# FNet and gated MLP on one core: the order of the last units of work, and when eight early chunks are split

## The chip, the cores and the metric

The kernel runs on one core of a Trainium2 chip. TensorE (PE) multiplies matrices, VectorE (DVE), ScalarE (ACT) and GpSimd (POOL) work on elements, and SyncE (SP) issues nearly all DMAs, in the order of its queue. PE writes into PSUM, which DVE and ACT read and GpSimd does not use here. The metric is device microseconds; the figure of merit is the median over several runs, here three for the kernel before.

## The reference, cut to what matters

```python
def _A_ref(x, dft_seq_re, dft_seq_im, dft_hid_re, dft_hid_im):
    a = jnp.einsum("bsd,ed->bse", x, dft_hid_re)
    b = jnp.einsum("bsd,ed->bse", x, dft_hid_im)
    return jnp.einsum("ts,bse->bte", dft_seq_re, a) - jnp.einsum("ts,bse->bte", dft_seq_im, b)

def _B_ref(x, w_gate, w_up, w_down):
    g = jnp.einsum("bsd,df->bsf", x, w_gate)
    u = jnp.einsum("bsd,df->bsf", x, w_up)
    h = _gelu(g) * u
    return jnp.einsum("bsf,fd->bsd", h, w_down)

h = x + _A_ref(_layernorm(x), ...)      # x is 1 x 2048 x 448, f32
h2 = h + _B_ref(_layernorm(h), ...)     # w_gate, w_up 448 x 1792, w_down 1792 x 448
```

Everything is f32 at the boundary. The change touches the second line alone, and in it the product of the gated hidden values with `w_down`, called "down" here.

## The kernel before, in words

Every f32 product is made from f16 halves: an operand is split into a high part (ACT rounds it to f16, `hi_part`, line 108) and a low part (DVE subtracts the high part from the value, `lo_part`, line 112), and PE runs three matmuls, high by high, high by low and low by high. On top of that the two products of the MLP use a seven-product scheme for 2 x 2 blocks, so that sums of blocks have to be formed before they are split.

The MLP runs in 42 **units** t = 0 to 41 of gate and up (`GateUp`), each for 128 of the 1792 hidden columns. Units 0 to 13 are for the first half of the rows, 14 to 27 for the third quarter and 28 to 41 for the last quarter. A unit accumulates in three PSUM banks, X, Y and Z, and its products are `x1`, `z1`, `y1`, `x2`, `z2`, `y2` and last `y3`, each 5 or 6 matmuls. `y3` is issued when the next unit has begun. Behind `z2`, `y2` and `y3` stands one DVE instruction each (lines 1076, 1084, 1089) that takes the sum out of its bank and so releases the bank. `c_last` is a Gelu on ACT and a product on GpSimd (line 1104). The hidden values of two neighbouring units lie in one SBUF tile `hs` of eight 128-column blocks, which `store` (line 1114) writes to DRAM after the odd unit, in the course of the next even one, or, for the last unit, after the loop.

Down runs in 56 **chunks** d = 7p + n. Group p = 0 to 7 stands for 256 rows of the output, and n = 0 to 6 for 256 hidden columns, those of the units 2n and 2n + 1 of a block. A chunk goes through: `hid_load` (SP reads it from DRAM into one of six tiles), `dn_sums` (three DVE instructions, lines 1174 to 1176), `dn_hi` (two on ACT), `dn_lo` (two on DVE), and `dn_mm` (21 matmuls, line 1212). The first of the two instructions of `dn_hi` and of `dn_lo` takes the chunk itself (128x256), the second its sums (128x640). Seven chunks accumulate in four PSUM banks. Then the group is **drained**: ACT copies two banks (`copy`, line 940), DVE adds four products from the others (`bank2`, `bank3`, line 944), GpSimd adds eight times from the copies (`sums`, line 972), and `dn_store` writes the 256 rows out (line 1230).

All of it is written out by hand, in one order per engine. The units 14 to 41 carry one or two chunks each (`steps`), so that in unit t the chunks of t are multiplied, those of t + 1 are split (`ahead`) and those of t + 2 are loaded and summed (`far`). The last two groups, p = 6 and 7, need hidden values of the units 28 to 41 themselves. Eight of their chunks are split during the units, into spare SBUF (`homes`): chunk `EARLY[t]` is loaded and summed in unit t - 1 and split in unit t + 1. The other six, 47, 48 and 52 to 55, are prepared just in time behind the loop, in the list `jit`, between the multiplications of the tail. Chunks 48 and 55 are made of the units 40 and 41. In the **tail**, PE multiplies chunks 42 to 52 one after the other, 11 times 21 matmuls, then products 0 to 6 of the chunks 53, 54 and 55, with DVE's last additions and the last stores between them.

What is scarce around the change: the accumulators of group 6 lie in the banks X, tr, Z and Y that the units leave, and the last three matmuls of a chunk go to Y (`dn_banks`, line 1195). Those of group 7 lie in the four banks of group 5. Chunks 47, 52 and 55 get one of three `dn_w` tiles, and 48, 53 and 54 one of two `raw` tiles, so that chunk 54 takes the place of chunk 48. A drain writes two tiles `v`, of which there is one set. At the end of unit 41 chunk 41 is multiplied, `y3` follows, and then the tail begins.

## Time and profile before

| | |
|---|---|
| median of three runs | 716.69 us (715.38 to 717.17) |
| time of the profiled execution | 715.99 us |
| span of the profiled execution | 714.2 us, 1.79 us less than its time |
| granted TensorE clock, mean | 0.997 |
| PE busy | 704.4 us, 99% of the span |
| DVE busy | 531.1 us, 74% |
| ACT, POOL busy | 353.0 us, 118.6 us |

The prediction quotes answers of the trace. A row of the timeline is start, duration, engine, line, operation, output<-input, shapes and count, and in square brackets the idle time of the engine before it with what ended it. PE rows of neighbouring matmuls of one kind are merged. A row of a table by window is the window, its length, the busy time and count for PE, PEld (weight load), DVE, ACT and POOL, then the granted clock, the busy share of the DMA engines and GB/s. A row of the waits is who waited for whom, the total, the number of times and the longest. A few matmul records are missing from the trace, so that counts can be short by some.

### The profile page before, as it was taken

The page shows a single profiled execution, that of the slowest core. Times are in us where ns is not written, and L with a number is a line of the kernel's source. Part 1 is how long each engine was busy: PE and PEld are TensorE (multiplying, and loading weights), DVE is VectorE, ACT ScalarE, POOL GpSimd, SP SyncE. Part 2 cuts the span into 40 slices and gives each one's busy share as a digit, 9 for nine tenths or more (in the row PEclk, how much of TensorE's full clock was granted, in tenths as well). Part 3 has the DMA queues.
Part 4 walks back from the last instruction along what each step waited for, and adds up shares of the span by engine and source line. Part 5 has one row for each costly group of instructions (what it writes and reads, how often), then busy time and mean ns, then how long its engine had stood idle before and what let it go on. Part 6 is the DMA issues. An engine that isn't in the chain of part 4 may idle for free.

```text
span 714.2 us, 13037 instructions
## 1 busy us (share of the span) xinstructions
PE 704.4 (99%) x4952; PEld 481.0 (67%) x4952; DVE 531.1 (74%) x1136; ACT 353.0 (49%) x656; POOL 118.6 (17%) x128
## 2 busy tenths in 40 slices
PE   9999999999999999999999999999999999999987
PEld 5555555555555555897644444479999999999877
DVE  7997648486858679998648787567688785989874
ACT  5776524163526354553527565554545544556421
POOL 0000000000000000000223333311231422334532
PEclk9999999999999999999999999999999999999999
DMA  7787538999988969552746858796898966878331
GB/s 271 250 248 264 113 135 240 235 311 247 235 299 248 243 214 266 216 137 86 191 159 225 289 193 193 198 339 229 226 310 244 278 243 231 314 266 312 121 116 52
DMA packets 116463, 160.47 MB, mean 225 GB/s; under 512 B 62000, under 2 KB 80560, under 8 KB 116400
## 3 DMA queue, kind: packets, MB, share of 16 engines
q1 hardware_dynamic: 116400, 159.64, 73.7%
q8 instruction: 38, 0.62, 0.4%
q14 instruction: 25, 0.20, 0.1%
HBM read 110.85 MB, written 34.87 MB: 204 GB/s over the span
## 4 chain that ended last, share of the span: by engine, by line
PE 97%; DVE 2%; DMA 1%; ACT 0%; issue 0%; SPq 0%; DVEq 0%
PE acc L648 33%; PE acc_d L1212 15%; PE pY L1010 14%; PE pZ L1010 9%; PE pX L1010 9%; PE y L714 9%; PE acc_f L520 7%; DMA wr<-in_w_seq_dram 1%; DVE dn_s L1175 0%; DVE dn_xs L112 0%; DVE hr L1476 0%; DVE hr L944 0%; DVE dn_s L1174 0%; DVE dn_s L1176 0%; DVE hs L1089 0%; ACT ws L108 0%
## 5 line engine op out<-in xcount | busy, mean ns | idle before, releaser
L648 PE MATMUL acc<-xs,ws 128*128 128x448 f16 x1248 | 237.9, 352 | 0.4 <-ACT ws L108 0.4
L648 PEld LDWEIGHTS <-ws 128*128 128x128 f16 x1248 | 122.0, 98 | 114.4 <-ACT ws L108 0.5
L1010 PEld LDWEIGHTS <-gw 128*128 128x128 f16 x1365 | 133.4, 98 | 42.9
L1212 PE MATMUL acc_d<-wd,dn_w 128*128 128x224 f16 x1008 | 111.0, 259 | 1.2 <-DVE dn_w L112 1.2
L1212 PEld LDWEIGHTS <-dn_w 128*128 128x128 f16 x1008 | 96.7, 98 | 3.7 <-DVE dn_w L112 1.7
L1104 POOL TENSOR_TENSOR hs<-hs,c 128x256 f32<-128x256 f32 (+1 forms) x42 | 53.6, 1277 | 226.7 <-ACT c L1102 159.1
L1010 PE MATMUL pY<-hops,gw 128*128 128x256 f16 (+1 forms) x595 | 89.9, 294 | 0.0
L114 DVE SCALAR_TENSOR_TENSOR ws<-wr,ws 128x1024 f16<-128x1024 f32 (+2 forms) x66 | 75.1, 1141 | 10.0 <-ACT ws L108 9.9
L108 ACT ACTIVATE ws<-wr 128x1024 f16<-128x1024 f32 (+2 forms) x66 | 63.8, 981 | 23.0 <-DMA wr<-in_w_seq_dram 21.9
L220 POOL TENSOR_TENSOR wd_s<-wd 128x448 f32<-128x448 f32 x7 | 9.4, 1349 | 343.3 <-DMA wd<-in_w_down_dram 342.5
L714 PE MATMUL y<-wh,z 128*128 128x448 f16 x336 | 66.2, 352 | 0.0
L1010 PE MATMUL pX<-hops,gw 128*128 128x256 f16 (+1 forms) x385 | 61.7, 294 | 0.0
L1010 PE MATMUL pZ<-hops,gw 128*128 128x256 f16 (+1 forms) x385 | 61.7, 294 | 0.0
L714 PEld LDWEIGHTS <-z 128*128 128x128 f16 x336 | 32.9, 98 | 30.1
L520 PEld LDWEIGHTS <-ws 128*128 128x128 f16 x504 | 48.3, 98 | 0.9
L1010 PEld LDWEIGHTS <-gu_w 128*128 128x128 f16 x273 | 26.6, 98 | 31.9 <-issue 0.3
L1055 ACT ACTIVATE pY<-pX 128x256 f32<-128x256 f32 (+1 forms) x42 | 18.4, 439 | 59.7 <-PE pX L1010 59.3
L1020 DVE SCALAR_TENSOR_TENSOR c<-pZ,u 128x256 f32<-128x256 f32 (+1 forms) x42 | 21.4, 510 | 34.6 <-PE pZ L1010 21.5
L1066 ACT ACTIVATE u<-pY 128x256 f32<-128x256 f32 (+1 forms) x42 | 19.1, 454 | 54.6 <-PE pY L1010 54.5
L972 POOL TENSOR_TENSOR hr<-hr,v 128x224 f32<-128x224 f32 x56 | 42.5, 785 | 16.7 <-ACT v L940 16.2
L112 DVE TENSOR_TENSOR dn_w<-dn_s,dn_w 128x640 f16<-128x640 f32 x48 | 43.1, 898 | 2.2 <-ACT dn_w L108 2.1
L108 ACT ACTIVATE dn_w<-dn_s 128x640 f16<-128x640 f32 x48 | 34.9, 728 | 18.9 <-DVE dn_s L1176 18.9
(133 smaller groups left out, 880.4 us busy)
## 6 DMA issues: line engine op xcount, KB each, us to landing
gw<-w_dram SPq DMA_DIRECT2D x35, 896.0 KB, 5.7
wr<-in_w_seq_dram SPq DMA_DIRECT2D x100, 256.0 KB, 4.5
hid_dram<-hs SPq DMA_DIRECT2D x28, 512.0 KB, 6.3
hid<-hid_dram SPq DMA_DIRECT2D x56, 256.0 KB, 5.7
w_dram<-gu_w SPq DMA_DIRECT2D x14, 896.0 KB, 5.7
gu_raw<-in_w_gu_dram SPq DMA_DIRECT2D x28, 384.0 KB, 5.8
wr<-in_w_seq_dram SPq DMA_DIRECT2D x14, 512.0 KB, 4.7
x<-in_x_dram SPq DMA_DIRECT2D x16, 224.0 KB, 2.7
```

The lines of the kernel that those rows point to most:

```text
L108: A.activation(dst, src, AF.Copy, scale=scale)
L112: V.tensor_sub(dst, src, hi)
L114: V.scalar_tensor_tensor(dst, src, scale, hi, op0=ALU.mult, op1=ALU.subtract)
L520: PE.matmul(fast_sum(n, k), fast_a(n, i, lw, a), fast_b(j, lx, b), start=j == 0 and m == 0 and k % 2 == 0, stop=j == NT // 2 - 1 and m == ...
L648: PE.matmul(acc[key][:, :D], w[:, lw, block * P : (block + 1) * P], xs[c][:, lx, :], start=c == 0 and m == 0, stop=c == NT - 1 and m == 2,)
L714: PE.matmul(y[:, :D], z[p][:, lz, k, g * P : (g + 1) * P], wh[:, lw, k, :], start=k == 0 and m == 0, stop=k == 6 and m == 2,)
L972: op(x, x, m)
L1010: PE.matmul(ps, w[:, wl, wa + ws, :], ops[:, m + ms, :], start=first and n == 0, stop=last and n == len(terms) - 1, skip_group_check=True,)
L1020: V.scalar_tensor_tensor(dst, ps, SC, other, op0=ALU.mult, op1=ALU.add)
L1066: A.activation(self.u2, self.Y, AF.Copy, scale=SC)
L1104: G.tensor_mul(c22, c22, self.cols(self.c12))
L1212: PE.matmul(ps, w[:, la, a, :], wd[n][:, lb, b, :], start=n == 0 and m == 0 and opens, stop=n == NC - 1 and m == 2, skip_group_check=True,)
```

## The change

It has four parts.

1. **The end of unit 41.** The drain of group 5 is not started in unit 41, and the splitting of chunk 46's low part, which stood ahead of `y3` on DVE, comes behind it. The sums of chunk 47 stay ahead of it.
2. **Chunks 48 and 55** are no longer stored and loaded back. `hid_in` of the two points into the `hs` tile of units 40 and 41. The last `store` and two `hid_load` are gone. `hid_load` of 53 and 54 moves from the tail into unit 41, behind that of 47 and 52. In `jit`, 48 now stands ahead of 52.
3. **The drain of group 5** (two copies on ACT, four additions on DVE) is issued behind the fourth chunk of the tail, and its eight GpSimd additions with the store behind the fifth. Before, the copies and additions of DVE stood in unit 41, and the GpSimd additions behind the first two chunks.
4. **EARLY.** Chunk 43 goes from 35 to 34, 50 from 36 to 35, 44 from 37 to 36, 51 from 39 to 37. Chunks 42, 49, 45 and 46 stay.

```diff
-    EARLY = {32: 42, 33: 49, 35: 43, 36: 50, 37: 44, 38: 45, 39: 51, 40: 46}
+    EARLY = {32: 42, 33: 49, 34: 43, 35: 50, 36: 44, 37: 51, 38: 45, 40: 46}
...
-        for d in far + ([52] if t + 1 == N_GU else []):
+        for d in far + ([52, 53, 54] if t + 1 == N_GU else []):
             hid_load(d)
...
         ends = now[-1] % NC == NC - 1
+        ends = ends and t + 1 < N_GU
         if ends:
...
-            if t + 1 < N_GU:
-                cur.z1()
+            cur.z1()
         prev.c_last()
         for d in ahead[1:]:
             dn_lo(d)
-        if split is not None:
+        if split is not None and t + 1 < N_GU:
             dn_lo(split)
...
     prev.y3()
-    prev.store()
-    hid_load(48)
-    jit = (47, 52, 48, 53, 54, 55, None)
+    hid_in[48], hid_in[55] = [hs[N_GU - 1][:, 4 * k : 4 * k + 4] for k in range(2)]
+    jit = (47, 48, 52, 53, 54, 55, None)
+    dn_lo(EARLY[N_GU - 2])
     for i, d in enumerate(range(6 * NC, 7 * NC + 4)):
         dn_mm(d)
-        if i == 0:
-            drains[5].sums(range(4))
         if i < 6:
             dn_hi(jit[i])
             dn_lo(jit[i])
             if jit[i + 1]:
                 dn_sums(jit[i + 1])
-        if i == 1:
-            drains[5].sums(range(4, 8))
-        if i < 3:
-            hid_load(53 + i)
-        if i == 2:
+        if i == 3:
+            drains[5] = dn_drain(5)
+            drains[5].copy()
+            drains[5].bank2()
+            drains[5].bank3()
+        if i == 4:
+            drains[5].sums(range(8))
             dn_store(5)
```

## Prediction, made before the changed kernel was built or run

> **What bounds the kernel now.** I read the page first, then the chain of waits of PE, then tables by window around each wait, and last the timeline of the engine that PE waited for.

> ```profile
> PE 704.4 (99%) x4952; PEld 481.0 (67%) x4952; DVE 531.1 (74%) x1136; ACT 353.0 (49%) x656; POOL 118.6 (17%) x128
> PE acc_d L1212 <- DVE hs L1089: 3.4, 1, 3.4
> PE acc_d L1212 <- DVE dn_w L112: 1.2, 1, 1.2
> ```

> PE is busy for 99% of the span, so an edit that leaves its matmuls alone can win only what PE waits, and these are the two waits in the part that the change touches. Around the longer one:

> ```profile
> 682.40:683.30 0.90, 0.90 (x10) 0.90 (x10) 0.90 (x2) 0.66 (x2) 0.90 (x3) 1.00 0.15 59
> 683.35:686.70 3.35, 3.35 (x21) 2.73 (x19) 2.88 (x6) 0.74 (x1) 1.15 (x1) 0.50 0.39 146
> ```

> After the wait the granted clock is 1.00 for 0.9 us, then 0.50 for 3.35 us. At half clock half of that is lost, 1.7 us. The wait therefore costs 3.36 + 1.7 = 5.06 us. The shorter one leaves the clock at 1.00:

> ```profile
> 667.00:670.00 3.00, 1.83 (x19) 1.46 (x17) 3.00 (x9) 2.23 (x6) 0.69 (x1) 1.00 0.36 141
> ```

> Why PE waited shows in the end of unit 41:

> ```profile
> 674.83 0.42 DVE L1020 SCALAR_TENSOR_TENSOR hs<-pY,m 128x256 f32<-128x256 f32 x1 [0.20 <-PE pY L1010]
> 676.48 1.61 DVE L944 SCALAR_TENSOR_TENSOR hr<-acc_d,hr 128x224 f32<-128x224 f32 x4 [1.23 <-PE acc_d L1212]
> 676.57 0.71 PE L1010 MATMUL pY<-hops,gw 128*128 128x256 f16 x5
> 677.12 1.89 PE L1212 MATMUL acc_d<-wd,hops 128*128 128x224 f16 x18
> 677.58 6.91 POOL L972 TENSOR_TENSOR hr<-hr,v 128x224 f32<-128x224 f32 x8
> 678.45 1.28 DVE L112 TENSOR_TENSOR dn_xs<-dn_s,dn_xs 128x640 f16<-128x640 f32 x1
> 679.65 0.88 DVE L1174 TENSOR_TENSOR dn_s<-hid 128x256 f32<-128x256 f32 x1
> 681.90 0.41 DVE L1089 SCALAR_TENSOR_TENSOR hs<-pY,g 128x256 f32<-128x256 f32 x1
> 682.37 3.76 PE L1212 MATMUL acc_d<-wd,hops 128*128 128x224 f16 x24 [3.36 <-DVE hs L1089]
> 683.90 0.87 DVE L1174 TENSOR_TENSOR dn_s<-hid 128x256 f32<-128x256 f32 x1
> ```

> `y3` ends at 677.3, but its DVE instruction, which releases bank Y, runs at 681.90. Ahead of it on DVE stand the drain of group 5, the low part of chunk 46 and the sums of chunk 47, these two slowed by the eight GpSimd additions (1.28 us for a form that takes 0.83 below). PE does 18 matmuls of chunk 42 and waits for Y until 682.37. The last row is for the pace under GpSimd work: a chunk takes 683.90 - 679.65 = 4.25 us on DVE.

> **The change, part by part.** *End of unit 41.* Ahead of `y3` on DVE only the sums of chunk 47 are left. Their price and the tail's pace come from a stretch in which GpSimd does nothing:

> ```profile
> 692.44 0.42 DVE L1174 TENSOR_TENSOR dn_s<-hid 128x256 f32<-128x256 f32 x1
> ...
> 693.31 0.42 DVE L112 TENSOR_TENSOR dn_w<-hid,dn_w 128x256 f16<-128x256 f32 x1
> 694.20 0.83 DVE L112 TENSOR_TENSOR dn_w<-dn_s,dn_w 128x640 f16<-128x640 f32 x1 [0.47 <-ACT dn_w L108]
> 694.94 0.42 DVE L1174 TENSOR_TENSOR dn_s<-hid 128x256 f32<-128x256 f32 x1
> ```

> Sums cost 0.87 us from start to start (692.44 to 693.31), a low part alone 0.42 + 0.83, at most 1.25 us, and a whole chunk just in time 2.50 us (692.44 to 694.94). The load of 47 must have landed, and it waits for the store of units 38 and 39:

> ```profile
> 668.14 0.32 SPq L1114 DMA_DIRECT2D hid_dram<-hs  x1
> 670.86 0.32 SPq L1127 DMA_DIRECT2D hid<-hid_dram  x1
> DMA to landing us min/median/max: 2.6/2.7/2.9
> ```

> It lands near 673.6 and does not delay them. So DVE takes sums 47 from 675.2 to 676.1 (677.0 if the GpSimd product of unit 41 doubles them), `y3` from 677.3 to 677.7, and Y is wanted at 677.12 + 1.89 = 679.0. The whole 5.06 us go; 1.3 us of DVE delay are in reserve.

> *Chunks 48 and 55 from SBUF, loads earlier.* A 512 KB store and two 256 KB loads go, 53 and 54 are issued on SP behind 52 with nothing queued behind them but the store of group 5. No wait of PE for these loads is in the chain of waits, so this gives nothing by itself. The sums of 48 now wait for `y3` and for GpSimd's product, both done by 678.

> *Tail.* Let PE start chunk 42 at 677.0 and do a chunk in 2.01 us:

> ```profile
> 696.64 0.42 ACT L108 ACTIVATE dn_w<-hid 128x256 f16<-128x256 f32 x1 [2.47 <-PE acc_d L1212]
> 698.40 2.17 PE L1212 MATMUL acc_d<-wd,dn_l 128*128 128x224 f16 x21
> 700.41 2.18 PE L1212 MATMUL acc_d<-wd,dn_xs 128*128 128x224 f16 x21
> ```

> DVE: low 46 to 678.9, low 47 to 680.1, then 2.50 us each for 48, 52 and 53 to 687.6, sums 54 to 688.5, the drain's 1.6 us (the L944 row) to 690.1. PE wants 47 at 687.0, 48 at 689.1, and group 5's banks for chunk 49 from 677.0 + 7 x 2.01 = 691.1 on, the fourth 18 matmuls (1.7 us) later. The moved drain is hidden with 1.0 us in hand. ACT then waits with `dn_hi(54)` until chunk 48 has freed its tile, as in the 696.64 row; behind it stand `dn_hi(55)` and the drain of group 6, in the old order too. From 691.1 two chunks take 5.0 us, or 8.5 at the pace under GpSimd work: chunk 55 is ready at 696.1 to 699.6 and wanted at 699.1 + 0.6. The eight GpSimd additions of group 5 (6.91 us before) run from 688 to at most 695, ahead of group 6's copies near 696, which need the same `v`. The tail costs nothing, and what follows PE's last matmul stays as it is.

> *EARLY.* Per unit, DVE gets the sums of 43 in unit 33 and its low part in unit 35; it loses sums in unit 38 and a low part in unit 40; the units between swap one chunk for another. DVE has no room early:

> ```profile
> 618.80:634.70 15.90, 15.88 (x155) 14.75 (x154) 15.90 (x33) 8.67 (x22) 7.84 (x11) 1.00 0.79 290
> 618.92 2.99 POOL L972 TENSOR_TENSOR hr<-hr,v 128x224 f32<-128x224 f32 x4
> 619.16 0.87 DVE L1175 TENSOR_TENSOR dn_s<-hid 128x256 f32<-128x256 f32 x1
> 620.62 0.41 DVE L1089 SCALAR_TENSOR_TENSOR hs<-pY,g 128x256 f32<-128x256 f32 x1
> 629.92 0.41 DVE L112 TENSOR_TENSOR dn_w<-hid,dn_w 128x256 f16<-128x256 f32 x1
> 630.39 0.31 PEld L1212 LDWEIGHTS <-dn_w 128*128 128x128 f16 x4 [0.27 <-DVE dn_w L112]
> 642.98 0.42 DVE L1020 SCALAR_TENSOR_TENSOR c<-pZ,u 128x256 f32<-128x256 f32 x1 [1.39 <-ACT dn_w L108]
> ```

> DVE is busy for all of 618.80 to 634.70, and chunk 32's low part (629.92) already holds PE's weight load at 630.39. The sums of 43 would stand at 620.62. They cost 0.87 us, or 1.9 if the GpSimd additions double them as they do at 619.16. One thing more can hold them: the load of 43 must wait for the store of units 30 and 31.

> ```profile
> 606.80 0.37 SPq L1114 DMA_DIRECT2D hid_dram<-hs  x1
> hid_dram<-hs SPq DMA_DIRECT2D x1, 512.0 KB, 7.7
> hid<-hid_dram SPq DMA_DIRECT2D x1, 256.0 KB, 7.1
> ```

> SP stands at that load until 614.5 (next in its queue is a load that issues at 616.78 anyhow), and the data lands 2.6 (the row above) to 7.1 us later, at 617.1 to 621.6: a wait of 0 to 1.0 us. All of it reaches chunk 32, since DVE has no gap on the way. PE loses 0.9 to 2.9 us near 630. I take 1.4, a half contended sum and no wait for the load. The low part of 43 in unit 35 (1.25 us) comes after chunk 32; the gap of 1.39 us at 642.98 takes it, and PE is itself later by then.

> Around the long wait the clock fell 0.9 us after PE had resumed (the 682.40 row), so a stretch in which PE still did something was idle enough. [...]

> *The wait at 668.* It is DVE's too:

> ```profile
> 654.01 3.37 POOL L1104 TENSOR_TENSOR hs<-hs,c 128x256 f32<-128x256 f32 x1 [6.48 <-ACT c L1102]
> 657.54 0.43 DVE L1020 SCALAR_TENSOR_TENSOR c<-pZ,u 128x256 f32<-128x256 f32 x1 [0.41 <-ACT dn_w L108]
> 658.20:670.80 12.60, 12.60 (x24) 1.00 0.47 161
> ```

> The sums dropped from unit 38 stood before 657.54, where DVE had caught up with PE, so they do not move what follows; from 658.20 DVE's work is the same. What they do is free GpSimd: its product took 3.37 us beside them, and the additions behind it, which slow DVE in unit 39, start earlier by a part of that. The wait of 1.17 us shrinks by 0 to 1.17; I take 0.7.

> **Sum**: 5.06 - 1.4 + 0.7 = 4.4 us less. Against the profiled execution's own time, 715.99 us, this is 711.6, against the median of three, 716.69, 712.3. I forecast 711.9, with 709.9 (5.06 - 0.9 + 1.17 off the profile, and the 0.7 us between profile and median once more) to 714.5 (5.06 - 2.9 off the median) as the likeliest case's own range.

> **Rivals.** *A, the new stall near 630 halves the clock.* A wait of 1.17 us did not; the one of 3.36 did, with at most 2.5 us of it in the 3.4 us before the fall. About 1.6 us lies between. Price 1.7 us: 713.6. *B, a new wait takes the old one's place: the drain of group 5 is late at chunk 49.* At 4.25 us a chunk, 48, 52 and 53 end at 692.9, the sums of 54 at 694.5 and the drain at 696.1. PE, which wants the fourth bank at 692.8, loses 3.3 us and 1.7 by the clock: 716.9. It decides once the drain ends after 692.8. For it speaks that the old tail did go at that pace; against it, that GpSimd's additions made it so, and they now come behind the drain. *C, slower, the change does not do what it says: the sums of 47 hold `y3`.* They stay ahead of it on DVE, and behind two transfers in a row. At the longest landings shown above the store of 668.14 lands 7.7 us and the load 7.1 us later, at 682.9, and Y is free after 0.87 + 0.41 us at 684.2. PE waits 5.2 us from 679.0, and 1.7 for the clock: 718.8. It decides once the load lands after 677.7. Against it: the store took 2.7 us there (668.14 to 670.86), the load as much, and the loads added stand behind it. *D, more gained*: DVE has more slack early than I see, and both short waits vanish: 5.06 + 1.17 + 0.27 off 716.3 (between the two bases) gives 709.8.

> **How the numbers follow.** The forecast has 0.69, A 0.10, B 0.07, C 0.06, D 0.08. About 0.3% (2.1 us) is what a measurement here tells from no change. Faster takes the forecast, D and half of A, 0.81; same the rest of A and most of B, 0.12; slower C and a little of B, 0.07. The range of 709.7 to 715.2 holds the forecast, A and most of D, and leaves out B and C.

> **What would show it.** PE's wait for line 1089 is gone and the clock stays 1.00 to the end; a PE wait for a low part of 1 to 2.5 us stands near 630; the wait near 668 is shorter than 1.17. The forecast is wrong if a wait of PE stands at chunk 42, 49 or 53 to 55, or if the clock falls before PE's last matmul.

## The result, and the profile after

| | before | after |
|---|---|---|
| median of five runs | 717.17 us (715.38 to 717.68) | 713.15 us (712.10 to 714.47) |
| profiled execution | 715.99 us | 712.20 us |
| its span | 714.2 us | 710.2 us |
| PE waits for line 1089 | 3.36 us, and 1.7 by the clock | none |
| PE waits near 630 and near 668 | 0.02 and 1.17 us | 1.67 and 0.69 us |

The ratio is 0.9947, with a 95% interval of 0.9928 to 0.9966: 2.4 to 5.2 us less, 4.0 by the spans. The forecast was 711.9 us, 4.4 us less than the profiled execution before.

The page of the changed kernel (busy time and share of each engine):

```profile
PE 703.0 (99%) x4952; PEld 480.1 (68%) x4952; DVE 531.8 (75%) x1136; ACT 353.2 (50%) x656; POOL 119.6 (17%) x128
```

And its waits (who waited for whom, in total, times, the longest); these two rows are all that PE has:

```profile
PE acc_d L1212 <- DVE dn_w L112: 2.4, 2, 1.7
PE pw L102 <- POOL sign_t L93: 1.4, 1, 1.4
```

PE's 4952 matmuls are the old ones, so what changed for PE are its waits and its clock. The 1.4 us lie at the start, in both kernels. What is left in the units are two waits for a low part, 1.67 and 0.69 us. The windows over the end of unit 41 and the tail, and over the wait near 630:

```profile
676.00:690.00 14.00, 14.00 (x148) 13.94 (x147) 11.68 (x26) 5.45 (x11) 2.31 (x3) 1.00 0.08 28
690.00:706.00 16.00, 16.00 (x170) 16.00 (x168) 10.56 (x26) 2.95 (x6) 9.48 (x15) 1.00 0.18 66
630.57:632.24 1.67, 0.00 (x1) 0.01 (x1) 1.67 (x7) 1.67 (x5) 0.00 (x0) 1.00 0.70 258
```

From 676 to 706, nearly to its last matmul, PE is busy without a gap at a clock of 1.00. Near 630 PE stands still for 1.67 us while DVE is busy throughout, and the clock stays. In the kernel before, the same place cost PE 0.02 us (0.92 busy of 0.94), for the weight load that it needs came just in time (630.39):

```profile
630.01:630.95 0.94, 0.92 (x10) 0.65 (x8) 0.94 (x2) 0.69 (x2) 0.00 (x0) 1.00 0.97 361
```

The timeline of the changed kernel shows why PE waits, first in the units:

```profile
619.12 3.44 POOL L972 TENSOR_TENSOR hr<-hr,v 128x224 f32<-128x224 f32 x4
620.83 0.41 DVE L1174 TENSOR_TENSOR dn_s<-hid 128x256 f32<-128x256 f32 x1
621.16 0.88 DVE L1175 TENSOR_TENSOR dn_s<-hid 128x256 f32<-128x256 f32 x1
622.63 0.41 DVE L1089 SCALAR_TENSOR_TENSOR hs<-pY,g 128x256 f32<-128x256 f32 x1
...
631.77 0.41 DVE L112 TENSOR_TENSOR dn_w<-hid,dn_w 128x256 f16<-128x256 f32 x1
632.24 0.56 PE L1212 MATMUL acc_d<-wd,dn_w 128*128 128x224 f16 x4 [1.67 <-DVE dn_w L112]
...
655.86 2.49 POOL L1104 TENSOR_TENSOR hs<-hs,c 128x256 f32<-128x256 f32 x1 [6.47 <-ACT c L1102]
658.32 2.63 POOL L972 TENSOR_TENSOR hr<-hr,v 128x224 f32<-128x224 f32 x4
670.49 0.56 PE L1212 MATMUL acc_d<-wd,dn_w 128*128 128x224 f16 x4 [0.69 <-DVE dn_w L112]
```

The sums of 43 take from 620.83 to 622.63, 1.80 us, doubled by the GpSimd additions of 619.12. Chunk 32's low part then stands at 631.77, 1.85 us later than before (629.92). PE's wait grows by 1.67 - 0.02 = 1.65 us; the other 0.20 us are a shift that PE has too, whose rows ahead of the wait are as much later (629.56 for 629.36). Near 655 the GpSimd product takes 2.49 us where it took 3.37, and the wait near 670 is 0.69. Then the tail:

```profile
676.53 0.42 DVE L1174 TENSOR_TENSOR dn_s<-hid 128x256 f32<-128x256 f32 x1
678.48 4.19 PE L1212 MATMUL acc_d<-wd,hops 128*128 128x224 f16 x42
678.75 0.42 DVE L1089 SCALAR_TENSOR_TENSOR hs<-pY,g 128x256 f32<-128x256 f32 x1 [0.73 <-PE pY L1010]
688.46 3.13 POOL L972 TENSOR_TENSOR hr<-hr,v 128x224 f32<-128x224 f32 x4 [10.93 <-ACT v L940]
688.73 0.88 DVE L1174 TENSOR_TENSOR dn_s<-hid 128x256 f32<-128x256 f32 x1
691.00 1.53 DVE L944 SCALAR_TENSOR_TENSOR hr<-acc_d,hr 128x224 f32<-128x224 f32 x4
692.57 2.18 PE L1212 MATMUL acc_d<-wd,hops 128*128 128x224 f16 x21
697.04 0.82 DVE L112 TENSOR_TENSOR dn_w<-dn_s,dn_w 128x640 f16<-128x640 f32 x1 [0.47 <-ACT dn_w L108]
```

The DVE instruction of `y3` (678.75) now waits for PE and no longer for other work on DVE. It releases Y at 679.2; PE wants it at 678.48 + 1.89 = 680.4. The moved drain runs at 691.00 to 692.53, just ahead of chunk 49 at 692.57. Chunk 55 is ready at 697.9.

By these rows the change is worth 5.06 - 1.65 + 0.48 = 3.9 us, and the spans say 4.0.

### The profile page after: what moved, and what is told of

Its sections match the earlier page's. It is cut to its first block, busy times and chain, and to the rows that moved or that the text cites. A ratio compares the mean times of both kernels' runs of the same rounds, so it can differ in the third digit from the quotient of the medians.

```text
span 710.2 us, 13038 instructions
## 1 busy us (share of the span) xinstructions
PE 703.0 (99%) x4952; PEld 480.1 (68%) x4952; DVE 531.8 (75%) x1136; ACT 353.2 (50%) x656; POOL 119.6 (17%) x128
## 4 chain that ended last, share of the span: by engine, by line
PE 95%; DVE 3%; DMA 1%; issue 0%; POOL 0%; SPq 0%; DVEq 0%; POOLq 0%
PE acc L648 33%; PE acc_d L1212 14%; PE pY L1010 14%; PE y L714 9%; PE pZ L1010 9%; PE pX L1010 9%; PE acc_f L520 7%; DMA hid<-hid_dram 1%; DVE dn_s L1175 1%; PE pw L102 1%; DVE dn_s L1174 0%; DVE dn_s L1176 0%; DVE dn_w L112 0%; DVE hops L112 0%; DVE hr L1476 0%
## 5 line engine op out<-in xcount | busy, mean ns | idle before, releaser
L1010 PEld LDWEIGHTS <-gw 128*128 128x128 f16 x1365 | 133.4, 98 | 42.9
L1212 PE MATMUL acc_d<-wd,dn_w 128*128 128x224 f16 x1008 | 111.2, 259 | 2.4 <-DVE dn_w L112 2.4
L1212 PEld LDWEIGHTS <-dn_w 128*128 128x128 f16 x1008 | 96.7, 98 | 5.2 <-DVE dn_w L112 3.2
L1104 POOL TENSOR_TENSOR hs<-hs,c 128x256 f32<-128x256 f32 (+1 forms) x42 | 55.3, 1316 | 225.1 <-ACT c L1102 150.3
L1010 PE MATMUL pY<-hops,gw 128*128 128x256 f16 (+1 forms) x595 | 89.9, 294 | 0.0
L108 ACT ACTIVATE ws<-wr 128x1024 f16<-128x1024 f32 (+2 forms) x66 | 63.8, 981 | 21.5 <-DMA wr<-in_w_seq_dram 20.8
L1010 PE MATMUL pX<-hops,gw 128*128 128x256 f16 (+1 forms) x385 | 61.7, 294 | 0.0
L1010 PE MATMUL pZ<-hops,gw 128*128 128x256 f16 (+1 forms) x385 | 61.7, 294 | 0.0
L1020 DVE SCALAR_TENSOR_TENSOR c<-pZ,u 128x256 f32<-128x256 f32 (+1 forms) x42 | 21.4, 510 | 37.8 <-PE pZ L1010 22.3
L1010 PEld LDWEIGHTS <-gu_w 128*128 128x128 f16 x273 | 26.6, 98 | 31.9 <-issue 0.2
L972 POOL TENSOR_TENSOR hr<-hr,v 128x224 f32<-128x224 f32 x56 | 41.8, 772 | 14.7 <-ACT v L940 13.8
L108 ACT ACTIVATE dn_w<-dn_s 128x640 f16<-128x640 f32 x48 | 35.0, 729 | 18.0 <-DVE dn_s L1176 18.0
L112 DVE TENSOR_TENSOR dn_w<-dn_s,dn_w 128x640 f16<-128x640 f32 x48 | 41.6, 867 | 2.0 <-ACT dn_w L108 1.9
## 6 DMA issues: line engine op xcount, KB each, us to landing
wr<-in_w_seq_dram SPq DMA_DIRECT2D x100, 256.0 KB, 4.5
hid_dram<-hs SPq DMA_DIRECT2D x27, 512.0 KB, 5.9
hid<-hid_dram SPq DMA_DIRECT2D x54, 256.0 KB, 5.6
wr<-in_w_seq_dram SPq DMA_DIRECT2D x14, 512.0 KB, 5.2
```

What stands on the lines that cost most here:

```text
L108: A.activation(dst, src, AF.Copy, scale=scale)
L112: V.tensor_sub(dst, src, hi)
L972: op(x, x, m)
L1010: PE.matmul(ps, w[:, wl, wa + ws, :], ops[:, m + ms, :], start=first and n == 0, stop=last and n == len(terms) - 1, skip_group_check=True,)
L1020: V.scalar_tensor_tensor(dst, ps, SC, other, op0=ALU.mult, op1=ALU.add)
L1104: G.tensor_mul(c22, c22, self.cols(self.c12))
```

## The experiments

Kernels of one group ran on one chip beside the same runs of the kernel before. "Changed" is the kernel of the result; each diff is against it unless another is named. All of them leave the computation as it is. The kernels with repeats do some sums several times over and write the same values.

### Is EARLY a loss by itself, and is the tail's gain whole without it?

The group's kernel before had a median of 716.63 us (714.75 to 719.50). The changed kernel once more, as the base:

> The changed kernel as it is, on the chip of the next three, so that they can be compared with it. Its trace had a span of 710.2 us with two waits of PE, 1.67 us near 632 and 0.69 us near 670. Both theories expect the same here: a span of 710 to 712 us, ratio to before 0.993 to 0.997, clock 1.00.

Measured: 713.53 us (712.78 to 713.88), ratio 0.995 (0.9937 to 0.9963), span 711.0, the waits 1.66 and 0.69 us.

The changed kernel with the old EARLY:

```diff
-    EARLY = {32: 42, 33: 49, 34: 43, 35: 50, 36: 44, 37: 51, 38: 45, 40: 46}
+    EARLY = {32: 42, 33: 49, 35: 43, 36: 50, 37: 44, 38: 45, 39: 51, 40: 46}
```

> The changed kernel with the old EARLY. Theory: the early units cost 1.67 - 0.21 = 1.46 us near 630 and give back 1.17 - 0.69 = 0.48 us near 670, and have no part in the tail. So the wait near 630 falls to about 0.2 us, the one near 668 is 1.2 us again, no wait stands in the tail, the clock stays 1.00, and the span is about 709.2 us, 1.0 less than with the new EARLY. Rival: the new EARLY takes work off VectorE in units 38 and 40 and thereby makes the room that the end of unit 41 needs; then a wait of 0.5 us or more stands at chunk 42, and the span is not below 710.2.

Measured: 711.45 us (711.08 to 712.33), ratio 0.9924 (0.9911 to 0.9937), span 709.8. The one wait for a low part that is left, in the timeline:

```profile
670.12 0.56 PE L1212 MATMUL acc_d<-wd,dn_w 128*128 128x224 f16 x4 [1.17 <-DVE dn_w L112]
```

The wait near 630 is gone and the one near 668 is back at its old 1.17 us. The other three parts alone gain 716.63 - 711.45 = 5.2 us (4.5 to 6.4 by the interval), and the first term of the sum was 5.06. EARLY gives back 2.1 us by the medians, 1.2 by the spans; the waits make 1.65 - 0.48 = 1.17 (the expectation took the old wait near 630 as 0.21 us; it is 0.02). The span with the old EARLY also holds a wait of 0.63 us for ACT near 349, in a part that EARLY does not touch and that half of the profiled executions here show. So some 0.7 to 0.9 us of what EARLY costs here are not explained by the two waits.

And the kernel before with the new EARLY alone:

> The kernel before with the new EARLY alone. Theory: span 714.2 + 1.46 - 0.48 = 715.2 us, about 1.0 us slower than before; the wait of 3.4 us for line 1089 and the half clock behind it stay. Rival: with less to do in units 38 and 40 VectorE reaches the last gated product earlier, the long wait shrinks by 1 us or more, and the span is 714 us or less.

Measured: 718.00 us (715.59 to 720.01, 12 runs), ratio 1.0021 (1.0007 to 1.0035): slower, by 0.5 to 2.5 us. Its profiled execution was the fastest of its twelve, and its trace holds something that no theory had. The wait for line 1089 is the old one:

```profile
616.57 4.27 POOL L1104 TENSOR_TENSOR hs<-hs,c 128x256 f32<-128x256 f32 x1 [4.83 <-ACT c L1102]
619.31 0.41 DVE L1174 TENSOR_TENSOR dn_s<-hid 128x256 f32<-128x256 f32 x1
631.50 0.56 PE L1212 MATMUL acc_d<-wd,dn_w 128*128 128x224 f16 x4 [0.99 <-DVE dn_w L112]
682.98 2.46 PE L1212 MATMUL acc_d<-wd,hops 128*128 128x224 f16 x24 [3.35 <-DVE hs L1089]
```

but the clock, by windows, stays at 1.00 behind it:

```profile
677.94:681.35 3.41, 1.69 (x18) 1.53 (x16) 3.31 (x6) 0.00 (x0) 3.33 (x5) 1.00 0.01 2
681.35:684.77 3.42, 1.79 (x19) 1.79 (x19) 3.42 (x6) 1.04 (x2) 3.42 (x5) 1.00 0.31 113
684.77:688.18 3.41, 3.41 (x38) 3.41 (x37) 2.32 (x5) 0.74 (x1) 0.34 (x1) 1.00 0.13 48
```

So the 1.7 us are not a fixed price of this wait. The section on the clock below goes on from here. In this trace the wait near 630 is 0.99 us and not 1.67: the sums of 43 ran undoubled, 619.31 to 620.18, while GpSimd's product took 4.27 us, where it took 2.52 in the trace of the changed kernel. The neighbour that yields was the other one this time.

### Which part of the tail removes the wait?

The group's kernel before: 717.22 us (714.68 to 719.51). First the drain of group 5 back in unit 41, its GpSimd additions behind the first two chunks:

```diff
-        ends = ends and t + 1 < N_GU
...
-            cur.z1()
+            if t + 1 < N_GU:
+                cur.z1()
...
-        if i == 3:
-            drains[5] = dn_drain(5)
-            drains[5].copy()
-            drains[5].bank2()
-            drains[5].bank3()
-        if i == 4:
-            drains[5].sums(range(8))
+        if i < 2:
+            drains[5].sums(range(4 * i, 4 * i + 4))
+        if i == 2:
```

> The changed kernel with the drain of group 5 back at the end of unit 41 (its GpSimd additions again behind the first two chunks of the tail); the low part of chunk 46 stays behind the last gated product, chunks 48 and 55 stay in SBUF. Theory: the drain's four additions hold VectorE until 679.4 (on the clock of the changed kernel's trace), the sums of 47 follow until 680.3, or 681.2 if GpSimd doubles them, and the last gated product's instruction ends at 680.7 to 681.6 where bank Y is wanted at 680.2: a wait of 0.5 to 1.4 us at chunk 42, no half clock, time 0.5 to 1.4 us above the changed kernel's. Rival: the low part of 46 was what held the product, so with it out of the way the drain may stay; no wait at chunk 42 and the same time.

Measured: 714.93 us (713.62 to 716.55), ratio 0.9965 (0.9945 to 0.9984). DVE's and PE's rows:

```profile
679.33 1.61 DVE L944 SCALAR_TENSOR_TENSOR hr<-acc_d,hr 128x224 f32<-128x224 f32 x4 [1.23 <-PE acc_d L1212]
680.86 0.51 DVE L1174 TENSOR_TENSOR dn_s<-hid 128x256 f32<-128x256 f32 x1
682.75 0.41 DVE L1089 SCALAR_TENSOR_TENSOR hs<-pY,g 128x256 f32<-128x256 f32 x1
683.22 2.46 PE L1212 MATMUL acc_d<-wd,hops 128*128 128x224 f16 x24 [1.36 <-DVE hs L1089]
```

The drain alone brings back 1.36 us of the wait, and the clock stays 1.00. A part of that is not the drain's own time: GpSimd's additions come back with it, at 680.43 in the same trace, and the sums of 47 beside them take 1.89 us (680.86 to 682.75) in place of 1.49. Second, the low part of 46 ahead of `y3` again:

```diff
-        if split is not None and t + 1 < N_GU:
+        if split is not None:
...
-    dn_lo(EARLY[N_GU - 2])
```

> The changed kernel with the low part of chunk 46 ahead of the last gated product again. Theory: VectorE is idle there for 0.81 us and the bank has 1.0 us more in hand, so 1.1 us of work (1.7 if GpSimd's product doubles it) fits: no wait at chunk 42, the same time within 0.3 us. Rival: each of the three pieces ahead of the product counts with its length, then a wait of 0.5 us or more appears at chunk 42.

Measured: 713.61 us (712.61 to 714.55), ratio 0.9947 (0.9927 to 0.9966), no wait at chunk 42. This edit alone is covered by the reserve: the low part fits by itself, and the drain does not. In the kernel before, both stand there, and the low part begins where the drain ends:

```profile
678.01 0.51 DVE L112 TENSOR_TENSOR dn_xs<-hid,dn_xs 128x256 f16<-128x256 f32 x1
```

It lasts to 679.65, 1.64 us, and the sums of 47 to 681.90, 2.25 us in place of 1.89. So 1.36 + 1.64 + 0.36 = 3.36 us: behind the drain nothing is left in reserve, and all that follows it counts in full.

Third, the store and the loads of 48 and 55, with the old order of the list:

```diff
-    hid_in[48], hid_in[55] = [hs[N_GU - 1][:, 4 * k : 4 * k + 4] for k in range(2)]
-    jit = (47, 48, 52, 53, 54, 55, None)
+    prev.store()
+    hid_load(48)
+    hid_load(55)
+    jit = (47, 52, 48, 53, 54, 55, None)
```

> The changed kernel with the hidden values of units 40 and 41 stored and chunks 48 and 55 loaded back from DRAM behind the last gated product, in the old order 47, 52, 48, 53, 54, 55; all else as changed. Theory: the store issues at 679.2, lands 2.7 to 4.8 us later and the load 2.7 to 3.8 us after that, at 684.6 to 687.8. VectorE, done with 52 at 684, waits with the sums of 48 for 1 to 4 us, and as the drain of group 5 stands two chunks behind them it ends at about 692 to 695 where chunk 49 wants the fourth bank at 694.3: a wait of PE of 0 to 1 us at chunk 49, time 0 to 1 us above the changed kernel's. Rival, as the prediction had it: the loads are hidden and give nothing by themselves; no wait at all and the same time.

Measured: 713.13 us (712.57 to 713.41), ratio 0.9942 (0.9927 to 0.9956), no wait of PE in the tail. The transfers do delay DVE and ACT, but ahead of work that has time:

```profile
685.57 0.42 DVE L1174 TENSOR_TENSOR dn_s<-hid 128x256 f32<-128x256 f32 x1 [1.35 <-DMA hid<-hid_dram]
```

The theory that they cost up to 1 us ends at zero within the noise; that these transfers are hidden, as the prediction had it, holds. The earlier loads of 53 and 54 were not taken back by themselves.

### Two waits that were left, and a faster version

The wait near 668 is DVE at the pace that GpSimd's additions leave it: with the old EARLY a low part of 128x640 takes 1.28 us beside them (663.91) and 0.81 behind them (669.99). The old EARLY, with group 4's eight additions moved to unit 40, where DVE has time (it idles for 3.37 us ahead of 673.28 in the trace of this kernel):

```diff
-    EARLY = {32: 42, 33: 49, 34: 43, 35: 50, 36: 44, 37: 51, 38: 45, 40: 46}
+    EARLY = {32: 42, 33: 49, 35: 43, 36: 50, 37: 44, 38: 45, 39: 51, 40: 46}
...
-            if p < 5 and t - t0 in (1, 2):
+            if p < 4 and t - t0 in (1, 2):
...
-            if p < 5 and t - t0 == 3:
+            if p == 4 and t - t0 == 3:
+                drains[p].sums(range(8))
+            if p < 5 and t - t0 == 3 + p // 4:
```

> As the run with the old EARLY, and the eight GpSimd additions of group 4 are moved from units 38 and 39 into unit 40, their store one unit later. Theory: the wait near 668 comes from these additions, which double VectorE's work in unit 39 (split and sums, some 3 us more), so it goes and the span is 709.2 - 1.2 = 708.0 us. Rival: VectorE has too much in unit 39 even without them, the wait stays at 0.5 us or more, or the additions now slow the sums of chunk 47 so that a wait of up to 1 us stands at chunk 42; span 709 us or more.

Measured beside the first group: 710.13 us (709.62 to 711.50), ratio 0.9906 (0.9892 to 0.9921), span 707.9. It is 1.3 us faster than the old EARLY alone, for a wait of 1.17. Behind the start PE has no wait at all any more in this trace. GpSimd's additions in their new place, in the timeline:

```profile
670.12 5.28 POOL L972 TENSOR_TENSOR hr<-hr,v 128x224 f32<-128x224 f32 x8
```

Once more, in the third group (kernel before 717.22, 714.15 to 719.84):

> The kernel with the old EARLY and the additions of group 4 moved to unit 40, again, beside the run above on the same chip. Both theories: no PE wait behind the start, 709.6 to 711.5 us.

Measured: 711.18 us (710.24 to 712.41), ratio 0.9926 (0.9901 to 0.9951). Its profiled execution has two waits of PE far from the change, 0.67 us near 350 and 0.16 near 480. This version beats both kernels. Then the same idea for the new EARLY, with group 3's additions in unit 36 and group 4's in unit 40:

```diff
-            if p < 5 and t - t0 in (1, 2):
+            if p < 3 and t - t0 in (1, 2):
...
-            if p < 5 and t - t0 == 3:
+            if (p, t - t0) in ((3, 4), (4, 3)):
+                drains[p].sums(range(8))
+            if p < 5 and t - t0 == (3, 3, 3, 5, 4)[p]:
```

> The changed kernel, new EARLY and all, with GpSimd's eight additions of group 3 moved from units 33 and 34 to unit 36 and those of group 4 from units 38 and 39 to unit 40, each store one or two units later. Theory: the new EARLY costs PE time only because GpSimd doubles VectorE's work in units 33, 34 and 39. Without that VectorE is some 4 us earlier at the low part of chunk 32 and 3 us earlier at that of chunk 40, so both waits near 632 and 670 are gone, no PE wait is left behind the start, and the time is that of the kernel with the old EARLY and the moved additions, 710 us. Rival: VectorE has too much to do in units 33 to 35 with the sums and the low part of 43 even alone; then a wait of 0.8 us or more stays near 632.

Measured: 712.42 us (711.85 to 713.73), ratio 0.9942 (0.9922 to 0.9961): the mechanism came out and the time did not. The sums of 43 are undoubled (621.04 to 621.91, 0.87 us) and both waits for a low part, near 630 and near 670, are gone. A new wait takes their place:

```profile
642.97 5.86 POOL L972 TENSOR_TENSOR hr<-hr,v 128x224 f32<-128x224 f32 x8
647.62 0.54 ACT L940 ACTIVATE v<-acc_d 128x448 f32<-128x448 f32 x1 [1.63 <-POOL hr L972]
648.22 0.73 PE L1212 MATMUL acc_d<-wd,dn_w 128*128 128x224 f16 x6 [1.49 <-ACT v L940]
```

There is one set of tiles `v`. The late additions of group 3 hold it, ACT's copies of group 4 wait, and PE waits for the bank that they read. The expectation had overlooked that.

### What does a wait cost by the clock?

To set the length of the wait, the sums of chunk 47 are done n more times ahead of `y3`, n = 4, 5 and 8:

```diff
+        if t + 1 == N_GU:
+            for _ in range(n):
+                h, s = dn_hid(47), dn_s[47]
+                V.tensor_add(s[:, 0:2], h[:, 0:2], h[:, 2:4])
+                V.tensor_sub(s[:, 2:4], h[:, 1:4:2], h[:, 0:4:2])
+                V.tensor_add(s[:, 4], h[:, 0], h[:, 3])
```

> The changed kernel with the three instructions of the sums of 47 issued four times more, with the same result, ahead of the last gated product: 4 x 0.87 = 3.5 us more work on VectorE at that place. Theory: 1.84 us of it fit (0.81 idle, 1.03 before the bank is wanted), so PE waits about 1.6 us at chunk 42, in one stretch; the clock stays at 1.00 since a stretch of 1.7 us left it there elsewhere; time 1.6 us above the changed kernel's. Rival: what decides the clock is the length of a wait alone with a limit somewhere between 1.2 and 1.6 us here, so the clock halves in this place and the time is 3.3 us above.

Measured: 714.44 us (713.92 to 714.80), ratio 0.996 (0.9948 to 0.9973), in the second group.

> The changed kernel with five repeats of the sums of 47 ahead of the last gated product (four gave a wait of 1.52 us and no fall of the clock). Wait 1.52 + 0.87 = 2.4 us. Theory: the clock falls when more than some share of one 3.41 us stretch of a fixed grid is idle, and that share lies between 1.73 us (no fall) and 2.45 us (fall). So a wait of 2.4 us halves the clock in a part of the executions at most, where nearly all of it lies in one stretch: times 715.9, or 717.6 with the fall. Rival: the length of the wait decides, with a limit between 1.67 and 3.35 us; then all executions are alike.

Measured: 716.73 us (715.45 to 717.79, 12 runs), ratio 1.000 (0.9986 to 1.0015), in the third group.

> The same with eight repeats: a wait of 1.52 + 4 x 0.87 = 5.0 us, of which at least 2.5 us lie in one stretch of 3.41 us whatever its phase. Theory: the clock falls in every execution and costs 1.7 us (3.4 where two stretches are idle enough): 713.5 + 5.0 + 1.7 = 720.2 us or more, with a spread no wider than that of a kernel without waits unless two stretches count. Rival, a stretch must be idle from end to end: with 5.0 us this holds in about half of the executions (1.6 of 3.4 us of phase), so the times fall into two groups, 718.5 and 720.2.

Measured: 720.16 us (719.76 to 722.91), ratio 1.006 (1.0038 to 1.0082), in the third group. PE's wait in the timeline, and then the windows from the start of the stretch that holds it, for four repeats:

```profile
682.38 1.79 PE L1212 MATMUL acc_d<-wd,hops 128*128 128x224 f16 x17 [1.52 <-DVE hs L1089]
```

```profile
679.89:683.30 3.41, 1.89 (x21) 1.72 (x19) 3.41 (x11) 1.04 (x2) 0.00 (x0) 1.00 0.00 0
683.30:686.71 3.41, 3.41 (x39) 3.41 (x37) 2.94 (x8) 1.04 (x2) 0.00 (x0) 1.00 0.03 7
```

The same two views for five:

```profile
683.82 4.12 PE L1212 MATMUL acc_d<-wd,hops 128*128 128x224 f16 x24 [2.40 <-DVE hs L1089]
```

```profile
680.73:684.14 3.41, 1.01 (x12) 0.85 (x10) 3.41 (x13) 0.68 (x2) 0.00 (x0) 1.00 0.01 2
684.14:687.55 3.41, 3.41 (x21) 2.77 (x19) 2.97 (x7) 1.11 (x4) 0.00 (x0) 0.50 0.02 5
```

And for eight:

```profile
685.41 4.64 PE L1212 MATMUL acc_d<-wd,hops 128*128 128x224 f16 x24 [5.02 <-DVE hs L1089]
```

```profile
680.62:684.03 3.41, 0.00 (x0) 0.00 (x0) 3.41 (x13) 0.00 (x0) 0.00 (x0) 1.00 0.00 0
684.03:687.45 3.42, 2.04 (x12) 1.66 (x12) 3.42 (x10) 1.04 (x2) 0.00 (x0) 0.50 0.02 5
687.45:690.86 3.41, 3.41 (x20) 2.79 (x19) 2.94 (x10) 1.04 (x2) 0.00 (x0) 0.50 0.00 0
```

The windows of the kernel before, cut in the same way:

```profile
679.92:683.33 3.41, 0.96 (x11) 0.96 (x11) 3.41 (x6) 1.04 (x2) 3.41 (x6) 1.00 0.04 17
683.33:686.74 3.41, 3.41 (x21) 2.79 (x19) 2.94 (x6) 0.74 (x1) 1.17 (x1) 0.50 0.39 144
```

In the three of these with a fall the clock changes at the ends of stretches of 3.41 us, which lie elsewhere in each execution (first change at 683.33, 684.14 and 684.03). It is halved for the next stretch where PE was idle for 2.40 us of a stretch (five repeats), 2.45 (before) or all of it (eight). It is not where PE was idle for 1.52 us (four repeats) or for 1.72 and then 1.63 (new EARLY alone, whose wait of 3.35 us was cut in two by a boundary). No change of the clock marks the stretches of the last two near the wait: their boundaries are an estimate, counted in the steps of 3.41 us of the other traces. So the bound, if the idle time of a stretch decides, lies between 1.72 and 2.40 us, an estimate from these five traces. With eight repeats the second stretch, idle for 1.38 us, was followed by half clock too: 2.04 us of work in it at half clock did not bring the clock back.

So four and five repeats, 0.88 us apart in PE's wait, are 2.3 us apart by the medians, though not on the same chip.

How often the clock falls can be read without a trace, because every execution of the experiments has its mean granted clock on record. One stretch at half clock takes 1.7 us of some 714, or 0.0024, off the mean. The traces give the scale: the mean is 0.999 or 1.000 where the clock did not fall, 0.997 with one such stretch (before, five repeats) and 0.995 with two (eight repeats). Executions by falls, each with its median time (0.998 counts as one):

| | none | one | two |
|---|---|---|---|
| kernel before, 50 | 18, 715.5 us | 26, 717.3 us | 6, 718.6 us |
| new EARLY alone, 12 | 2, 716.1 us | 10, 718.4 us | none |
| five repeats, 12 | 3, 715.8 us | 9, 717.2 us | none |
| eight repeats, 7 | none | none | 7, 720.2 us |

All other kernels here have 0.999 or 1.000 in every execution. So the fall does come in only a part of the executions with five repeats, as the theory had it, and the rival, by which all are alike, is out. It also bears on the new EARLY alone: with one fall each, it is 718.4 against 717.1 us for the nine such executions of the kernel before beside it, 1.3 us slower. Why the kernel before has two falls in 6 executions no trace shows.

## Why the prediction was right, and where it was off

- **The long wait, 5.06 us.** Right in its mechanism. The wait for line 1089 and the half clock are gone, and without EARLY the gain is 5.2 us. The price of the clock in it was right for the profiled execution, and the prediction took it as the wait's own. New EARLY alone shows an execution with the same wait and no fall, and of 50 executions of the kernel before 18 have none. That the profiled one has one is luck for the sum: without it the term would have been 3.36 us.
- **The reserve at `y3`, 1.3 us.** Measured 680.4 - 679.2 = 1.2. The sums of 47 take 1.5 us from start to end and are early enough; rival C, the late load, did not come.
- **EARLY, a new wait of 1.4 us.** Measured 1.67 - 0.02 = 1.65. The mechanism was right to the chunk, and nearly all of the delay reached PE, as the step had it. The size is low because the sums were doubled in full, 1.80 us, where the step took a half contended sum; the load did not hold them. New EARLY alone shows that this could have gone the other way (0.87 us).
- **The wait near 668, 0.7 us less.** This term is mis-sized too: 1.17 - 0.69 = 0.48. The product near 655 became 0.88 us shorter, as the step had it (3.37 to 2.49), and about half of that reached PE.
- **The tail costs nothing.** Right by its result, with a step that failed. The prediction had GpSimd's additions behind the drain in rival B and from 688 on in its own step, and it priced DVE's sums of 54 beside them as if GpSimd did nothing. They follow ACT's copies and began at 688.46, ahead of these sums and of the drain. The sums took 2.27 us (688.73 to 691.00) in place of 0.87. Carried to the later start of chunk 42, 678.48 in place of 677.0, the drain was to end at 691.6; it ended at 692.53, with 0.04 us in hand ahead of chunk 49 and not 1.0. PE wants the last bank 1.7 us later still, so it did not wait, and rival B stayed away by less than it seemed.
- **Chunks 48 and 55, nothing.** Right: with their transfers back the time is 713.13 us.
- **Rival A.** The new wait did not halve the clock: 1.67 us at a clock of 1.00. That a wait of this length leaves it alone was not shown when the forecast took it so. By an estimate it lay whole in one stretch of the clock, 629.27 to 632.69, which is 24 steps of 3.413 us back from that execution's change at 711.19, so 1.67 us idle is too little. PE would have had to wait up to 0.7 us longer, with all of it in one stretch, to reach the estimated bound between 1.72 and 2.40. The 3.4 us before the fall that the rival counts are in the trace of before 679.92 to 683.33, the last stretch at full clock, with 2.45 us of the wait in it. The rival's price, 1.7 us, is near what one fall costs the kernel before by the medians above, 717.3 - 715.5 = 1.8 us.
- **Rival D.** Both short waits can vanish, but not by this change: it took the old EARLY and another place for eight additions of GpSimd.

The sum was 4.4 us and came out as 3.9 by the terms. Of the 0.5 us, half is the wait near 630 and the rest the one near 668.

## What to carry to other kernels

Where an engine has no slack, as DVE in the units 32 to 34 here, work moved earlier is paid nearly in full by the next one who waits, even if the place it came from gains: price both ends from the rows there. Look at what slows the critical engine from beside it, here GpSimd's additions (a low part of 1.28 us for 0.81): moving those of one group to a unit in which DVE has time was worth 1.3 us, but moving another group's made a new wait of 1.5 us, since they held a tile that ACT needed. And bring PE's long waits below some 1.7 us first: waits of 1.52 and 1.67 us cost no clock in these traces, and with one of 2.40 us a second price came, in 9 of 12 executions.

## What was not expected of the hardware

**Which of DVE and GpSimd yields is not fixed.** With the same program up to there, the sums of one chunk took 0.87 us in one execution and 1.80 in another, and GpSimd's product 4.27 or 2.52 us (0.73 at 676.89 in the kernel before, where DVE drains from PSUM). With the sums at full pace `y3` was done 2.45 us earlier (620.18 for 622.63), but GpSimd's additions then came later and slowed the next low parts, so that only 0.74 us were left at chunk 32 (631.03 for 631.77), and the wait near 630 was 0.99 in place of 1.67 us. In the traces of the two kernels, the changed kernel once more, the old EARLY, the faster version and the moved additions of groups 3 and 4 that product took 2.52 us, and with the new EARLY alone 4.27; what decides which of the two yields is not shown. Among the rows here only DVE instructions with both inputs in SBUF were doubled (0.41 to 0.88 us for 128x256); those that read PSUM (the drain, 1.53 us for four beside the additions, 0.38 to 0.39 each with GpSimd busy or idle; line 1089, 0.41) were not.
